# Sorted block attention followed by a PReLU layer pair: three stages in turn, or one interleaved program

## The chip, the cores and the metric

The kernel runs on one core of one Trainium2 chip. The time is the device time of one execution in microseconds (us). A profile of one execution is available, and its span runs from the first to the last recorded instruction. TensorE multiplies matrices (PE in the profile, PEld for its weight loads), VectorE is DVE, ScalarE is ACT, GpSimd is POOL and SyncE is SP. Of a matrix product, the operand that is loaded into the array is called the weights here, and the other one, whose columns stream through, the moving operand.

## The reference

Four batches, 8 heads, 768 tokens in 8 blocks of 96, head dimension 64. A small 8x8 matrix per batch and head is normalised five times and mixes the blocks of k and v; each block of queries then attends to its own mixed block; the result goes through two dense layers with a PReLU between them.

```python
for _ in range(5):                       # sort_net: [4, 8, 8, 8]
    P = np.exp(P - P.max(-1)); P = P / (P.sum(-1) + 1e-9); P = P / (P.sum(-2) + 1e-9)
k_sorted = einsum('bhij,bhjcd->bhicd', P, k_b)        # the same for v
scores = q_b @ k_sorted.T / sqrt(64); attn = softmax(scores)   # per block of 96
x = (attn @ v_sorted) as [3072 tokens, 512]
h = x @ w_in                             # 512 -> 2048
out = (maximum(h, 0) + alpha * minimum(h, 0)) @ w_out # 2048 -> 512
```

## The kernel before

The program is three stages, one behind the other, each written as a fixed order of instructions per engine (`_Plan` keeps one list per engine; the order of the calls is the order of the queues).

1. Preparation. POOL issues the loads of q, k and v, which also turn f32 into bf16, in six halves into three staging buffers `stg`. The five normalisations run on DVE with one exponential on ACT each (L178 to L196); a DMA through `L2` (L200) and a mask build the block-diagonal mixing matrix `bd_bf`. TensorE transposes q (L323) into `psKV`; k and v are mixed first (L353, evacuated at L368 and L370 into `srt`) and transposed in a second pass (L323, L389). ACT and DVE evacuate into `QT`, `KT` (L337, L339) and `VS` (L402, L404).
2. Attention, in 32 groups of one batch and one block with all 8 heads: eight score products (L510, keys in the partitions), one exponential (L519), eight products with `VS` (L539), whose 65th column of ones gives the row sum, a reciprocal (L548) and a multiplication (L554) on DVE, four transposes (L572) and their copy into `xT` (L581). The loop staggers three groups. The softmax takes no maximum off.
3. The dense layers in 6 chunks of 512 tokens: `emit_phase1` has 16 steps of four 128x512 products (L655), a Relu on ACT (L663) scaled by 1 - alpha, which is right for alpha up to 1, and a combination on DVE (L672). `emit_phase2` has 4 tiles of 16 products (L699), an evacuation on ACT (L705) and a DMA out from SP (L711). Phase 1 of a chunk is put ahead of phase 2 of the chunk before.

Of the kernel before, what the change touches and what calls it, by code (L numbers as in the profile page):

```python
# [13 lines left out]
NB = 8  # L15
# [6 lines left out]
TOK_CHUNK = 512  # L22
N_CHUNKS = NT // TOK_CHUNK
TT_PER_CHUNK = TOK_CHUNK // 128
HALF_ELEMS = 128 * 6144
NSTG = 3


class _Stream:

    def __init__(self, sem):
        self.sem = sem
        self.v = 0


class _Plan:

    ENGS = ("pool", "sync", "pe", "act", "dve")

    def __init__(self):  # L40
        self.ops = {e: [] for e in self.ENGS}

    def op(self, eng, fn, stream=None, n=1):
        if stream is None:
            self.ops[eng].append(lambda e, fn=fn: fn(e))
            return None

        def _do(e, fn=fn, s=stream.sem, n=n):
            inst = fn(e)
            inst.then_inc(s, n)  # L50
        self.ops[eng].append(_do)
        stream.v += n
        return stream.v

    def wait(self, eng, stream, value):
        if value <= 0:
            return
        sem = stream.sem
        self.ops[eng].append(lambda e, sem=sem, value=value: e.wait_ge(sem, value))


def _emit(nc, P):
    with nc.Block() as blk:
        for eng_name, starter in (("pool", blk.gpsimd), ("sync", blk.sync), ("pe", blk.tensor),
                                  ("act", blk.scalar), ("dve", blk.vector)):
            fns = P.ops[eng_name]
            if not fns:
                continue

            def _run(e, fns=fns):  # L70
                for fn in fns:
                    fn(e)
            starter(_run)


def bass_sinkhorn_attn__then__act_prelu_kernel(
    nc: bass.Bass,
    q: bass.AP,
    k: bass.AP,
    v: bass.AP,  # L80
    sort_net: bass.AP,
    moe_w_in: bass.AP,
    moe_w_out: bass.AP,
    moe_alpha: bass.AP,
    out: bass.AP,
):
    _build(nc, q, k, v, sort_net, moe_w_in, moe_w_out, moe_alpha, out, debug=None)


def _build(nc, q, k, vin, sort_net, moe_w_in, moe_w_out, moe_alpha, out, debug=None):  # L90
    P = _Plan()
    es = ExitStack()

    def sem(name):
        return es.enter_context(nc.semaphore(name))

    st_sn = _Stream(sem("s_dma_sn"))
    st_alpha = _Stream(sem("s_dma_alpha"))
    st_l2dma = _Stream(sem("s_dma_l2"))
    st_lda = [_Stream(sem("s_dma_lda%d" % i0)) for i0 in range(NSTG)]  # L100
    st_ldb = [_Stream(sem("s_dma_ldb%d" % i0)) for i0 in range(NSTG)]
    st_win = _Stream(sem("s_dma_win"))
    st_wout = _Stream(sem("s_dma_wout"))
    st_outp = [_Stream(sem("s_out0")), _Stream(sem("s_out1"))]
    st_dbg = _Stream(sem("s_dbg"))
    st_pool = _Stream(sem("s_pool"))
    st_dve = _Stream(sem("s_dve"))
    st_act = _Stream(sem("s_act"))
    st_pe = _Stream(sem("s_pe"))

    identf = es.enter_context(nc.sbuf_tensor("identf", [128, 128], F32))
    identb = es.enter_context(nc.sbuf_tensor("identb", [128, 128], BF16))
    mask128 = es.enter_context(nc.sbuf_tensor("mask128", [128, 128], F32))
    ones128 = es.enter_context(nc.sbuf_tensor("ones128", [128, 128], F32))
    P32 = es.enter_context(nc.sbuf_tensor("P32", [32, 64], F32))
# [150 lines left out]
    def issue_load(L):  # L266
        buf = L % NSTG
        readers = v_stg_readers[buf]
        if readers > 0:
            P.wait("pool", st_pe, readers)  # L270
# [485 lines left out]
```

## Time and profile before

| what | value |
|---|---|
| median of 3 runs (lowest, highest) | 314.13 us (313.93, 315.18) |
| span of the profiled execution | 312.7 us |
| mean granted TensorE clock over the span | 0.896 |
| PE, PEld busy | 279.8 us, 165.2 us |
| DVE, ACT busy | 162.6 us, 162.0 us |
| POOL busy | 10.1 us |
| moved by DMA | 20.26 MB |

The profiled execution's time outside the profiler is not recorded beside its span; the median of the runs is 1.4 us above the span. An average share over the span hides that the three stages have different limits: each stage has to be read from its own stretch of the trace. The granted clock is the share of full speed that the throttle gives to TensorE; it has a row only from the first time that it is reported.

### The profile page before, as it was taken

What the parts mean: (1) busy time and instruction counts of PE and PEld (TensorE: products, weight loads), DVE (VectorE), ACT (ScalarE), POOL (GpSimd) and SP (SyncE); (2) the same over time, 40 slices, a digit from 0 to 9 for tenths busy, and PEclk for the clock granted to TensorE, in tenths of its full rate; (3) what the DMA queues carried; (4) which work ended last, traced back from release to release, by engine and by line L of the source; (5) the groups of instructions that cost most, each with busy time, mean ns of one, the idle gap of its engine ahead of it and who ended that gap; (6) DMA issues with size and microseconds to landing.
All of it is one profiled execution on the core that took longest, in us unless ns stands there. A gap on an engine that the chain in (4) does not pass through costs nothing.

```text
span 312.7 us, 4827 instructions
## 1 busy us (share of the span) xinstructions
PE 279.8 (89%) x1950; PEld 165.2 (53%) x1970; DVE 162.6 (52%) x286; ACT 162.0 (52%) x222; POOL 10.1 (3%) x23
## 2 busy tenths in 40 slices
PE   0486788786899999978999999999999999999995
PEld 0475366445788888863444444444444444444442
DVE  5604899897466666654888108504810860482000
ACT  2498787796444444433777137516722752572111
POOL 6010300000000000001000000000000000000000
PEclk9999999999655555556999999999999999999999
DMA  6999999600000000005900020011002001100121
GB/s 83 210 215 214 214 209 212 130 2 0 2 2 0 2 0 3 2 0 79 191 0 3 34 101 0 2 74 61 2 34 84 16 3 67 67 2 34 67 100 69
DMA packets 10198, 20.26 MB, mean 65 GB/s; under 512 B 3008, under 2 KB 5056, under 8 KB 9408
## 3 DMA queue, kind: packets, MB, share of 16 engines
q0 software_dynamic: 4320, 13.63, 22.7%
q1 hardware_dynamic: 5856, 6.32, 5.9%
q8 instruction: 16, 0.26, 0.3%
q14 instruction: 6, 0.05, 0.1%
HBM read 27.28 MB, written 6.29 MB: 107 GB/s over the span
## 4 chain that ended last, share of the span: by engine, by line
PE 79%; DVE 10%; DMA 4%; ACT 3%; issue 3%; POOL 0%; SPq 0%; DVEq 0%; POOLq 0%
PE psH L655 27%; PE psO L699 26%; PE pO L539 8%; PE psS L510 8%; DMA L<-P 4%; PE psT L572 3%; PE psKV L323 3%; DVE KT L339 2%; PE ps_sort L353 2%; DVE VS L404 2%; PE psKV L389 2%; DVE QT L339 1%; ACT srt L368 1%; ACT VS L402 1%; DVE xq L554 1%
## 5 line engine op out<-in xcount | busy, mean ns | idle before, releaser
L672 DVE SCALAR_TENSOR_TENSOR hT<-psH,alphaT,t 128x512 bf16<-128x512 f32 x96 | 72.1, 751 | 69.7 <-ACT t L663 59.6
L655 PE MATMUL psH<-xT,w_in_bf 128*128 128x512 bf16 x375 | 84.7, 384 | 1.3 <-issue 0.9
L699 PE MATMUL psO<-w_out_bf,hT 128*128 128x512 bf16 x377 | 83.3, 379 | 0.4
L663 ACT ACTIVATE t<-psH,omaT 128x512 bf16<-128x512 f32 x96 | 66.0, 687 | 24.2 <-PE psH L655 24.2
L655 PEld LDWEIGHTS psH<-xT,w_in_bf 128*128 128x128 bf16 x384 | 37.9, 99 | 47.2 <-issue 3.2
L699 PEld LDWEIGHTS psO<-w_out_bf,hT 128*128 128x128 bf16 x384 | 37.6, 98 | 45.3
L705 ACT ACTIVATE outstg<-psO 128x512 f32<-128x512 f32 x24 | 14.3, 597 | 68.1 <-PE psO L699 68.1
L519 ACT ACTIVATE Esb<-psS 96x768 bf16<-96x768 f32 x32 | 25.7, 806 | 34.9 <-PE psS L510 34.9
L323 PE MATMUL psKV<-identb,stg 128*64 128x128 bf16 x192 | 17.0, 255 | 15.0 <-DVE P L196 7.4
L510 PE MATMUL psS<-QT,KT 64*96 64x96 bf16 x256 | 26.8, 274 | 1.4 <-DVE VS L404 1.4
L539 PE MATMUL pO<-VS,Esb 96*96 96x65 bf16 x256 | 26.0, 266 | 2.0 <-DVE xq L554 1.4
L539 PEld LDWEIGHTS pO<-VS,Esb 96*96 96x96 bf16 x256 | 22.6, 188 | 5.8 <-issue 1.7
L510 PEld LDWEIGHTS psS<-QT,KT 64*96 64x96 bf16 x256 | 21.9, 181 | 5.8 <-ACT VS L402 1.5
L323 PEld LDWEIGHTS psKV<-identb,stg 128*64 128x64 bf16 x192 | 14.6, 134 | 17.3 <-DMA stg<-in_q_dram 11.8
L554 DVE TENSOR_TENSOR xq<-pO,rec 96x512 bf16<-96x512 f32 x32 | 22.0, 687 | 1.1
L548 DVE RECIPROCAL rec<-pO 96x8 f32<-96x8 f32 x32 | 6.5, 204 | 25.4 <-PE pO L539 25.4
L337 ACT ACTIVATE QT<-psKV 64x1024 bf16<-64x1024 bf16 x20 | 18.7, 1022 | 1.1 <-PE psKV L323 1.0
L572 PE MATMUL psT<-identb,xq 96*128 96x96 bf16 x128 | 16.3, 278 | 1.1 <-DVE xT L581 1.1
L353 PE MATMUL ps_sort<-stg,bd_bf 128*128 128x512 bf16 x44 | 13.5, 384 | 4.0 <-DVE bd_bf L221 1.7
L368 ACT ACTIVATE srt<-ps_sort 128x512 bf16<-128x512 f32 x24 | 13.8, 594 | 2.9 <-remote 1.8
L370 DVE CAST srt<-ps_sort 128x512 bf16<-128x512 f32 x24 | 14.7, 678 | 0.8 <-PE ps_sort L353 0.8
L339 DVE COPY KT<-psKV 64x1024 bf16<-64x1024 bf16 x12 | 14.3, 1220 | 1.4 <-PE psKV L323 0.6
(45 smaller groups left out, 127.1 us busy)
## 6 DMA issues: line engine op xcount, KB each, us to landing
out_dram<-outstg SPq DMA_DIRECT2D x24, 256.0 KB, 2.0
stg<-in_q_dram POOLq DMA_DIRECT2D x2, 1280.0 KB, 13.7
stg<-in_k_dram POOLq DMA_DIRECT2D x2, 1280.0 KB, 18.5
stg<-in_v_dram POOLq DMA_DIRECT2D x2, 1280.0 KB, 11.7
w_in_bf<-in_moe_w_in_dram POOLq DMA_DIRECT2D x1, 2048.0 KB, 22.0
w_out_bf<-in_moe_w_out_dram POOLq DMA_DIRECT2D x1, 2048.0 KB, 14.4
stg<-in_q_dram POOLq DMA_DIRECT2D x2, 256.0 KB, 8.2
stg<-in_k_dram POOLq DMA_DIRECT2D x2, 256.0 KB, 12.8
```

Source lines behind the costliest of these rows:

```text
L323: inst = e.matmul(AP(psKV, (hf * 64) * 3072 + pbuf * 1024 + t * 128, [[3072, 64], [1, 128]]), AP(src_t, c * 64, [[6144, 128], [1, 64]]), i ...
L339: vv = P.op(eng, lambda e, d=dstap, s=srcap: e.tensor_copy(d, s), stream)
L353: v_mm = P.op("pe", lambda e, m=m, hf=hf, buf=buf: e.matmul(AP(ps_sort, (m % 4) * 512, [[2048, 128], [1, 512]]), AP(bd_bf, hf * 128, [[256 ...
L510: inst = e.matmul(oap, lhsT, rhs)
L519: v_exp[g] = P.op("act", lambda e, gbuf=gbuf: e.activation(AP(Esb, gbuf * 768, [[1536, 96], [96, 8], [1, 96]]), AP(psS, gbuf * 1024, [[204 ...
L539: inst = e.matmul(oap, lhsT, rhs)
L554: v_nrm[g] = P.op("dve", lambda e, gbuf=gbuf: e.tensor_tensor(out=AP(xq, gbuf * 512, [[1024, 96], [64, 8], [1, 64]]), in0=AP(pO, 0, [[1024 ...
L572: inst = e.matmul(oap, lhsT, rhs, is_transpose=True)
L655: inst = e.matmul(oap, lhsT, rhs, start=(kt == 0), stop=(kt == KT_TILES - 1))
L663: v_relu = P.op("act", lambda e, ft=ft, hbuf=hbuf: e.activation(AP(t1, hbuf * TOK_CHUNK, [[4 * TOK_CHUNK, 128], [1, TOK_CHUNK]]), AP(psH, ...
L672: v_cmb[step] = P.op("dve", lambda e, ft=ft, hbuf=hbuf, hbase=hbase: e.scalar_tensor_tensor(out=AP(hT, hbase + ft * TOK_CHUNK, [[HT_ROW, 1 ...
L699: inst = e.matmul(oap, lhsT, rhs, start=(ft == 0), stop=(ft == FT_TILES - 1))
```

## The change

The whole kernel is rewritten. `_Graph` collects every operation with what it reads and writes, an estimated duration and a priority. A list scheduler at build time then fixes the order of each engine's queue: the engine that is free earliest takes the ready operation with the lowest priority number. Copies out of PSUM may go to ACT or DVE, whichever the scheduler finds free. Waits are emitted for dependencies that are not already known to be met.

- Work goes batch by batch. Group g has priority g; the dense layers of a chunk of groups (two chunks of 192 tokens, then seven of 384) get priorities just behind the chunk's last group, so that they are placed between later groups; the preparation of the next batch is placed between the groups of the present one.
- k and v are mixed and transposed by one product each: `prep_k` has the data as weights and the mixing matrix as moving operand, 64 rows by 64 columns, two heads in two halves of the array; `prep_v` takes every 64th element of a row as a weight. q is transposed 128 columns at a time and evacuated by four copies into `QTz`, where the other head's half is zero.
- All preparation products share one PSUM bank, `psP`; `psH` has two banks in place of four, `psY` one.
- The mixing matrix is spread by a product with a selection matrix instead of a DMA. The subtraction of the maximum stays in the first normalisation alone.
- Each group computes its scores twice: once with queries in the partitions for a row maximum on DVE (`s1` and `tensor_reduce`), once with keys in the partitions, with the negative maximum added by eight more products (`s2`).
- The PReLU is h + (1 - alpha) * relu(-h): Relu with a constant scale of -1 into an f32 tile, then the combination on DVE.
- POOL also zeroes parts of `QTz` and `VST`.

The core of the diff; most removed lines stand above in the kernel before:

```diff
-TOK_CHUNK = 512
-NSTG = 3
...
-class _Plan:
...
-    for it in range(5):
-        P.wait("dve", st_dve, st_dve.v)
-        v = P.op("dve", lambda e: e.reduce_max(rm[:, :], P3, axis=AxisListType.X), st_dve)
...
-        v_l2 = P.op("sync", lambda e, hf=hf: e.dma_start(
...
-    for g in range(NG + 2):
...
-    for tc in range(N_CHUNKS):
-        emit_phase1(tc)
...
+RING = 768
...
+XLAT = {"pe": 210, "act": 60, "dve": 60, "pool": 80, "sync": 80}
...
+def t_pe(*mms):
+    return sum(max(n, m, 64) / 2.4 + 4 for n, m in mms)
...
+def t_act(n, ptr=0):
+    return 100 + n / 1.2 + 93 * ptr
...
+def t_dve(n, mode=1):
+    return 120 + n / (0.96 * mode)
...
+            best = None
+            for e in ENGS:
+                if not ready[e]:
+                    continue
+                first = max(free[e], min(o.ready[e] for o in ready[e]))
+                op = min((o for o in ready[e] if o.ready[e] <= first), key=lambda o: (o.prio, o.idx))
+                if best is None or first < best[0]:
+                    best = (first, e, op)
+            at, e, op = best
...
+    psS = ps("psS", [128, 2, 512], F32)
+    psO = ps("psO", [128, 2, 512], F32)
+    psH = ps("psH", [128, 2, 512], F32)
+    psY = ps("psY", [128, 512], F32)
+    psP = ps("psP", [128, 512], F32)
...
+        for hp in range(2):
+            G.add(POOL, lambda e, hp=hp: e.memset(
+                AP(VST[0].bitcast(F32), (hp * 64 + 32) * 3072, [[3072, 32], [1, 3072]]), 0.0),
+                3200, w=[("VST", 0, 1, hp)], prio=-80)
+        for n in range(2):
+            for hp in range(2):
+                G.add(POOL, lambda e, hp=hp, n=n: e.memset(
+                    AP(QTz[n].bitcast(F32), (1 - hp) * 64 * 3072 + hp * 1536, [[3072, 64], [1, 1536]]), 0.0),
+                    1700, w=[("QTz0", n, hp)], prio=-79 + 40 * n)
...
+            if it == 0:
+                dv(lambda e: e.reduce_max(rm[:, :], P3, axis=AxisListType.X), ["P"], ["rm"])
+                dv(lambda e: e.tensor_tensor(out=P3, in0=P3, in1=bc(rm), op=AluOpType.subtract),
+                   ["P", "rm"], ["P"])
...
+    def spread_k(b, prio):
+        G.add(PE, lambda e: e.matmul(psP[:, 0:64], AP(selk, b * 128, [[512, 32], [1, 128]]),
+                                     P32[:, :]), 500, r=["P", "selk"], w=PSP, prio=prio)
+        G.add(DVE, lambda e: e.tensor_tensor(
+            out=AP(dtmp, 0, [[64, 128], [8, 8], [1, 8]]), in0=AP(psP, 0, [[512, 128], [8, 8], [1, 8]]),
+            in1=AP(mkj, 0, [[8, 128], [0, 8], [1, 8]]), op=AluOpType.mult), 210,
+            r=PSP + ["mkj"], w=["dtmp"], prio=prio)
+        G.add(DVE, lambda e: e.reduce_sum(dsel[:, :], AP(dtmp, 0, [[64, 128], [8, 8], [1, 8]]),
+                                          axis=AxisListType.X), 200, r=["dtmp"], w=["dsel"], prio=prio)
+        G.add(DVE, lambda e: e.tensor_tensor(
...
+    def prep_q(b, u, prio):
+        n = b % 2
+        def f(e):
+            inst = None
+            for p in range(8):
+                pr = 8 * u + p
+                inst = e.matmul(AP(psPb, p * 128, [[1024, 128], [1, 128]]),
+                                AP(QS[n], pr * 128, [[3072, 128], [1, 128]]),
+                                identb[:, :], is_transpose=True)
+            return inst
+        G.add(PE, f, t_pe(*[(128, 128)] * 8), r=[("QS", n), "identb"], w=PSP, prio=prio)
+        for cp in range(2):
+            for hp in range(2):
+                o = AP(QTz[n], hp * 64 * 6144 + hp * 3072 + cp + 16 * u,
+                       [[6144, 64], [96, 32], [48, 2], [2, 8]])
+                i = AP(psPb, cp * 64 * 1024 + hp * 64, [[1024, 64], [2, 32], [1, 2], [128, 8]])
+                G.add(EITHER, lambda e, o=o, i=i: copy(e, o, i), t_either(512),
+                      r=[("psP", cp), ("QTz0", n, hp)], w=[("QTz", n, u, cp, hp)], prio=prio)
+    def prep_k(b, u, prio):
+        n = b % 2
+        def f(e):
+            inst = None
+            for c in range(8):
+                cc = 8 * u + c
+                for hp in range(2):
+                    inst = e.matmul(AP(psP, hp * 64 * 512 + c * 64, [[512, 64], [1, 64]]),
+                                    AP(KS[n], hp * 64 * 3072 + cc * 64, [[3072, 64], [1, 64]]),
+                                    AP(BDK, hp * 64 * 512 + b * 128 + hp * 64, [[512, 64], [1, 64]]))
+            return inst
+        G.add(PE, f, t_pe(*[(64, 64)] * 16), r=[("KS", n), ("BDK", b)], w=PSP, prio=prio)
+        o = AP(KT[n], 8 * u, [[3072, 128], [96, 32], [48, 2], [1, 8]])
+        i = AP(psP, 0, [[512, 128], [2, 32], [1, 2], [64, 8]])
+        G.add(EITHER, lambda e: copy(e, o, i), t_either(512), r=PSP, w=[("KT", n, u)], prio=prio)
+    def prep_v(b, u, prio):
+        n, hf, b2 = b % 2, b // 2, b % 2
+        def f(e):
+            inst = None
+            for dd in range(8):
+                inst = e.matmul(AP(psP, dd * 64, [[512, 96], [1, 64]]),
+                                AP(VST[hf], 8 * u + dd, [[6144, 128], [64, 96]]),
+                                AP(BDV, hf * 128 + b2 * 64, [[256, 128], [1, 64]]))
+            return inst
+        G.add(PE, f, t_pe(*[(64, 96)] * 8),
+              r=[("VST", hf, x, y) for x in range(2) for y in range(2)] + [("BDV", hf, b2)],
+              w=PSP, prio=prio)
+        o = AP(VS[n], 8 * u, [[64 * 65, 96], [65, 64], [1, 8]])
+        i = AP(psP, 0, [[512, 96], [1, 64], [64, 8]])
+        G.add(EITHER, lambda e: copy(e, o, i), t_either(512), r=PSP + [("VS1", n)], w=[("VS", n, u)],
+              prio=prio)
...
+        vs_keys = [("VS", n, u) for u in range(8)]
+        banks_s, banks_o = ["psS0", "psS1"], ["psO0", "psO1"]
+        def s1(e):
+            inst = None
+            for s in range(8):
+                h4, hp = s // 2, s % 2
+                inst = e.matmul(AP(psS, (s // 4) * 512 + (s % 4) * 96, [[1024, 96], [1, 96]]),
+                                AP(QTz[n], hp * 3072 + h4 * 768 + i * 96, [[6144, 128], [1, 96]]),
+                                AP(KT[n], h4 * 768 + i * 96, [[3072, 128], [1, 96]]))
+            return inst
+        G.add(PE, s1, t_pe(*[(96, 96)] * 8), r=kt_keys + qt_keys, w=banks_s, prio=prio)
+        G.add(DVE, lambda e: e.tensor_reduce(
+            AP(nm[m], 0, [[8, 96], [4, 2], [1, 4]]), AP(psS, 0, [[1024, 96], [512, 2], [96, 4], [1, 96]]),
+            AxisListType.X, AluOpType.max, negate=True), t_dve(768), r=banks_s, w=[("nm", m)], prio=prio)
+        def s2(e):
+            inst = None
+            for h4 in range(4):
+                base = (h4 // 2) * 512 + (h4 % 2) * 192
+                e.matmul(AP(psS, base, [[1024, 96], [1, 192]]),
+                         AP(KT[n], h4 * 768 + i * 96, [[3072, 128], [1, 96]]),
+                         AP(QTz[n], h4 * 768 + i * 96, [[6144, 128], [3072, 2], [1, 96]]),
+                         start=True, stop=False)
+                for hp in range(2):
+                    inst = e.matmul(AP(psS, base + hp * 96, [[1024, 96], [1, 96]]),
+                                    AP(nm[m], 2 * h4 + hp, [[8, 96], [0, 96]]),
+                                    AP(identb, 0, [[128, 96], [1, 96]]), start=False, stop=(hp == 1))
+            return inst
+        G.add(PE, s2, t_pe(*[(192, 96), (96, 96), (96, 96)] * 4), r=kt_keys + qt_keys + [("nm", m), "identb"],
+              w=banks_s, prio=prio)
+        G.add(ACT, lambda e: e.activation(
+            AP(Esb[m], 0, [[768, 96], [384, 2], [1, 384]]), AP(psS, 0, [[1024, 96], [512, 2], [1, 384]]),
+            ACTF.Exp, scale=0.125), t_act(768), r=banks_s, w=[("Esb", m)], prio=prio)
+        def o(e):
+            inst = None
+            for s in range(8):
+                h4, hp = s // 2, s % 2
+                inst = e.matmul(AP(psO, hp * 512 + h4 * 68, [[1024, 96], [1, 65]]),
+                                AP(Esb[m], s * 96, [[768, 96], [1, 96]]),
+                                AP(VS[n], ((hp * 4 + h4) * 8 + i) * 65, [[64 * 65, 96], [1, 65]]))
+            return inst
+        G.add(PE, o, t_pe(*[(65, 96)] * 8), r=vs_keys + [("Esb", m)], w=banks_o, prio=prio)
+        G.add(DVE, lambda e: e.reciprocal(AP(rec[m], 0, [[8, 96], [4, 2], [1, 4]]),
+                                          AP(psO, 64, [[1024, 96], [512, 2], [68, 4]])), 200,
+              r=banks_o, w=[("rec", m)], prio=prio)
...
+        def tr(e):
+            inst = None
+            for kt in range(4):
+                inst = e.matmul(AP(psOb, 640 + kt * 96, [[2048, 128], [1, 96]]),
+                                AP(xq[m], kt * 128, [[512, 96], [1, 128]]),
+                                AP(identb, 0, [[128, 96], [1, 96]]), is_transpose=True)
+            return inst
+        G.add(PE, tr, t_pe(*[(96, 128)] * 4), r=[("xq", m), "identb"], w=["psO0"], prio=prio)
+        o2 = AP(xT, b * S + i * BLK, [[KT_TILES * NT, 128], [NT, 4], [1, 96]])
+        i2 = AP(psOb, 640, [[2048, 128], [96, 4], [1, 96]])
+        G.add(EITHER, lambda e: copy(e, o2, i2), t_either(384, 2), r=["psO0"], w=[("xT", g)], prio=prio)
...
+    def ffn1(ga, gb, ft, prio):
+        tok, n = ga * BLK, (gb - ga) * BLK
+        hb, tb = step[0] % 2, step[0] % 3
+        step[0] += 1
...
+        G.add(PE, f, t_pe(*[(n, 128)] * 4), r=[("xT", g) for g in range(ga, gb)] + [("w_in", ft // 4)],
+              w=[("psH", hb)], prio=prio)
+        G.add(ACT, lambda e: e.activation(AP(t1[tb], 0, [[384, 128], [1, n]]),
+                                          AP(psH, hb * 512, [[1024, 128], [1, n]]), ACTF.Relu, scale=-1.0),
+              t_act(n), r=[("psH", hb)], w=[("t1", tb)], prio=prio)
+        G.add(DVE, lambda e: e.scalar_tensor_tensor(
+            out=AP(hT, ft * RING + tok % RING, [[FT_TILES * RING, 128], [1, n]]),
+            in0=AP(t1[tb], 0, [[384, 128], [1, n]]), scalar=AP(omaT, ft, [[16, 128], [1, 1]]),
+            in1=AP(psH, hb * 512, [[1024, 128], [1, n]]), op0=AluOpType.mult, op1=AluOpType.add),
+            t_dve(n), r=[("psH", hb), ("t1", tb), "omaT"],
...
+    def ffn2(t, prios):
+        tok = t * 128
+        if t < 21:
+            bank, key, row = (psY, 0), "psY", 512
+        else:
+            bank, key, row = ((psS, (t % 2) * 512), "psS%d" % (t % 2), 1024)
+        ob = t % 4
...
+    for u in range(3):
+        prep_q(0, u, -50)
+    for b in range(4):
+        spread_k(b, -48 if b == 0 else 1.0 + b)
+        if b % 2 == 0:
+            spread_v(b // 2, -47 if b == 0 else 1.5 + b)
+        if b == 0:
+            for u in range(6):
+                prep_k(0, u, -46)
+            for u in range(8):
+                prep_v(0, u, -45)
...
+    chunks = [(0, 2), (2, 4)] + [(c, c + 4) for c in range(4, NG, 4)]
+    tile_done = 0
+    ffn_plan = []
+    for ga, gb in chunks:
+        w = gb - ga
+        v0 = gb + 0.5
+        for ft in range(FT_TILES):
+            ffn_plan.append((v0 + w * ft / FT_TILES, 0, (ga, gb, ft)))
+        last = gb * BLK // 128
+        nt = last - tile_done
+        for x in range(nt):
+            prios = [v0 + w + w * (x + p / 4) / nt for p in range(4)]
+            ffn_plan.append((prios[0], 1, (tile_done + x, prios)))
...
+        b, i = g // NB, g % NB
+        if i == 0 and b + 1 < B:
+            load_k(b + 1, 8 * b - 20)
+            if b != 2:
+                load_v(b + 1, 8 * b - 19)
+            if b == 1:
+                load_v(3, 8 * b - 17)
+            load_q(b + 1, 8 * b - 18)
+        attention(g, g)
+        if b + 1 < B:
+            units = ([(prep_k, u) for u in range(6)] + [(prep_v, u) for u in range(8)]
+                     + [(prep_q, u) for u in range(3)])
+            for x in range(len(units)):
+                if i == 1 + x * 7 // len(units):
+                    units[x][0](b + 1, units[x][1], 8 * b + 1 + x * 7 / len(units) - 2)
...
```

More of the change, by code (lines that the diff above doesn't have):

```diff
@@ L62, in _emit @@
[L62 to L73, printed above, removed]
+NG = B * NB
+RING = 768
+EPS = 1e-9
+XLAT = {"pe": 210, "act": 60, "dve": 60, "pool": 80, "sync": 80}
```

965 lines of the change are left out of this document (374 added, 591 removed).

## The prediction

> **What bounds the kernel now.** I read the page's first two parts, then the busy time by stretch with its clock, then the timeline at the borders of the stages. The columns of a stretch are its length, busy us (and instructions) of PE, PEld, DVE, ACT and POOL, granted clock, DMA share, GB/s.
>
> ```profile
> span 312.7 us, 4827 instructions
> PE 279.8 (89%) x1950; PEld 165.2 (53%) x1970; DVE 162.6 (52%) x286; ACT 162.0 (52%) x222; POOL 10.1 (3%) x23
> ...
> PEclk9999999999655555556999999999999999999999
> DMA  6999999600000000005900020011002001100121
> ...
> 0.00:19.30 19.30, 7.76 (x72) 7.52 (x73) 8.90 (x41) 9.11 (x14) 4.96 (x15) 1.00 0.89 160
> 19.30:79.00 59.70, 45.58 (x506) 30.70 (x508) 44.56 (x53) 47.80 (x59) 3.95 (x7) 1.00 0.71 143
> 79.00:141.00 62.00, 59.53 (x623) 51.36 (x624) 36.74 (x95) 24.82 (x31) 0.00 (x0) 0.51 0.01 1
> 141.00:145.50 4.50, 3.62 (x12) 1.42 (x12) 1.11 (x2) 0.76 (x2) 1.16 (x1) 0.50 0.23 25
> 145.50:309.60 164.10, 163.26 (x745) 74.17 (x758) 71.32 (x95) 78.95 (x119) 0.00 (x0) 1.00 0.18 50
> ```
>
> There are three limits. Preparation takes 79 us, with no engine full: the loads fill the DMA for seven slices of 7.8 us, and ACT and DVE evacuate. Attention takes 62 us with PE busy throughout, but at half the clock. The dense layers take 164 us at full clock with no gap. So 164 us can't shrink; what can is the 145 us ahead, in which TensorE is idle, small-grained or slow. The clock has no event before 19.3 us, so the 1.00 of the first stretch is no measurement; the durations say what it was:
>
> ```profile
> 13.46 6.50 PE L323 MATMUL psKV<-identb,stg 128*64 128x128 bf16 x64 [4.14 <-DMA stg<-in_q_dram]
> 20.17 0.47 PEld L323 LDWEIGHTS psKV<-identb,stg 128*64 128x64 bf16 x8 [0.38 <-ACT QT L337]
> 20.18 0.63 PE L323 MATMUL psKV<-identb,stg 128*64 128x128 bf16 x8 [0.22 <-ACT QT L337]
> 21.09 0.63 PE L323 MATMUL psKV<-identb,stg 128*64 128x128 bf16 x8 [0.28 <-ACT QT L337]
> 79.00 0.43 PEld L539 LDWEIGHTS pO<-VS,Esb 96*96 96x96 bf16 x8 [0.66 <-ACT Esb L519]
> ...
> 87.51 0.71 PEld L510 LDWEIGHTS psS<-QT,KT 64*96 64x96 bf16 x8
> ...
> 142.20 8.07 PE L655 MATMUL psH<-xT,w_in_bf 128*128 128x512 bf16 x29 [0.88 <-issue]
> ...
> L510 PEld LDWEIGHTS psS<-QT,KT x16: 116/122/122, 77.9 to 79.8; 64*96 64x96 bf16 x16
> ```
>
> At 13.46 us, 64 transposes take 0.102 us each; at 20.17 us eight loads take 0.47 us, about 0.05 each. The start runs at half clock too.
>
> **The change, part by part.** It makes one PE-bound program of the three, so the sum is: PE's work at full clock, plus the time before PE can be kept full, plus what it loses.
>
> *PE's work.* From the last stretch, a 512-column product costs 164.1/758 = 0.2165 us. Eight loads of 96 columns take 0.43 us, the last of them 0.122: (0.43 - 0.122)/7 = 0.044 each. A 128-column transpose is 0.05, a 192-column product 0.2165 x 192/512 = 0.081.
> - Dense layers: the same columns, 768 x 0.2165 = 166.3, and 192 more instructions by narrower chunks; I take 167 us.
> - Attention, per group: `s1` 8 x 0.044 = 0.35; `s2` 8 x 0.044 + 4 x 0.081 = 0.68 (this is the added pass for the maximum); output 0.35; transposes 4 x 0.05 = 0.20. Together 1.58, times 32 = 51 us. Before it was 62 us at half clock, so the doubled scores are paid by the clock, if the clock is full.
> - Preparation: q 96 x 0.05 = 5 us. k 384 products of 64x64: between 0.022 (two halves of the array at once) and 0.044 (the 96-column row); I take 0.035, 13.4 us (8.4 to 17). v 256 products, whose weights are every 64th element: between 0.044 and 0.084 ((0.71 - 0.12)/7, the same load at half clock, as the worst near row); I take 0.05, nearest to the contiguous row, 12.8 us (11.3 to 21.5). With the spreads 32 us. The old second pass of transposes for k and v goes.
>
> [...]
>
> PE total: 167 + 51 + 32 = 250 us.
>
> *The time until PE is full.* The dense layers can start when two groups are in `xT`.
>
> ```profile
> 2.82 0.21 DVE L178 TENSOR_REDUCE rm<-P 32x8 f32<-32x64 f32 x1
> 3.31 0.26 ACT L183 ACTIVATE P<-P 32x64 f32<-32x64 f32 x1 [1.22 <-DVE P L180]
> ...
> 14.01 0.26 DVE L196 TENSOR_TENSOR P<-P,cs 32x64 f32<-32x64 f32 x1
> ...
> 14.98 11.62 DMA L<-P
> ...
> L137 POOL MEMSET ones<- 128x128 f32 x1 | 0.2, 204 | 0.3 <-POOLq L741 0.3
> L741 POOL MEMSET const-float32-0.0<- 128x1 f32 x1 | 0.1, 98 | 0.3 <-issue 0.3
> 10.00:20.00 10.00, 6.50 (x64) 6.33 (x64) 3.21 (x15) 7.76 (x11) 0.00 (x0) 1.00 1.01 206
> 140.35 0.34 DVE L581 COPY xT<-psT 128x384 bf16<-128x384 bf16 x1
> 140.81 0.29 PEld L572 LDWEIGHTS psT<-identb,xq 96*128 96x128 bf16 x4 [1.24 <-DVE xT L581]
> 140.84 0.48 PE L572 MATMUL psT<-identb,xq 96*128 96x96 bf16 x4 [1.05 <-DVE xT L581]
> 141.36 0.36 DVE L581 COPY xT<-psT 128x384 bf16<-128x384 bf16 x1 [0.66 <-PE psT L572]
> L370 DVE CAST srt<-ps_sort 128x512 bf16<-128x512 f32 x24 | 14.7, 678 | 0.8 <-PE ps_sort L353 0.8
> L368 ACT ACTIVATE srt<-ps_sort 128x512 bf16<-128x512 f32 x24 | 13.8, 594 | 2.9 <-remote 1.8
> ```
>
> The normalisation ended at 14.3 us; four maxima and subtractions of 3.31 - 2.82 = 0.49 go, one short operation comes: 12.5 us. The 11.6 us of the `L` DMA, queued behind the loads, go. The loads of q, k, v of batch 0 are 2.36 MB, 11.5 us at 206 GB/s, now first in POOL's queue: in by 15 us. POOL's zeroing: 0.098 + 0.83 ns per column gives 2.65 us for 3072 and 1.4 us for 1536, so two and two end near 11.5 us, and the copies into `QTz` wait for them.
>
> From there one bank, `psP`, takes everything in turn, at half clock (sparse products did not raise it before). Bank free to first load: 0.12 us (140.69 to 140.81). Last product's tail plus hand-over: 0.25 (four products at 0.09 end at 141.32, the copy starts at 141.36). A copy of 512: 0.6 to 0.68. So a unit of k costs 16 x 0.06 + 0.37 + 0.64 = 1.97; of v 8 x 0.084 + 0.37 + 0.69 = 1.73; of q, with four copies on two engines, 8 x 0.102 + 0.37 + 1.28 = 2.5. One q unit waits for the zeroing and ends at 12.3; two more to 17.3; two spreads of 0.75 to 18.8; six of k to 30.6; eight of v to 44.5. Then two groups' output, scaling, transposes and copy, about 2.9 us each, in turn on `psO`: 50 us. At full clock the same chain is 2.1, 1.57 and 1.46 us a unit and 2.4 us a group: 44 us.
>
> By then PE has done a quarter of the preparation (8), three groups' scores (3), two groups' rest (1) and some units of batch 1 (1): 13. Left: 237 us.
>
> *What is lost behind 50 us.* The clock has to rise; before, it rose 3.3 us after dense products began (142.20 to 145.5), and I take 5 us at half, 2.5 lost (0 to 5). ACT and DVE must keep up:
>
> ```profile
> L672 DVE SCALAR_TENSOR_TENSOR hT<-psH,alphaT,t 128x512 bf16<-128x512 f32 x96 | 72.1, 751 | 69.7 <-ACT t L663 59.6
> L519 ACT ACTIVATE Esb<-psS 96x768 bf16<-96x768 f32 x32 | 25.7, 806 | 34.9 <-PE psS L510 34.9
> L554 DVE TENSOR_TENSOR xq<-pO,rec 96x512 bf16<-96x512 f32 x32 | 22.0, 687 | 1.1
> L548 DVE RECIPROCAL rec<-pO 96x8 f32<-96x8 f32 x32 | 6.5, 204 | 25.4 <-PE pO L539 25.4
> L581 DVE COPY xT<-psT 128x384 bf16<-128x384 bf16 x32 | 11.0, 344 | 0.7 <-PE psT L572 0.7
> L339 DVE COPY KT<-psKV 64x1024 bf16<-64x1024 bf16 x12 | 14.3, 1220 | 1.4 <-PE psKV L323 0.6
> L705 ACT ACTIVATE outstg<-psO 128x512 f32<-128x512 f32 x24 | 14.3, 597 | 68.1 <-PE psO L699 68.1
> 309.59 0.60 ACT L705 ACTIVATE outstg<-psO 128x512 f32<-128x512 f32 x1 [2.86 <-PE psO L699]
> out_dram<-outstg SPq DMA_DIRECT2D x24, 256.0 KB, 2.0
> ```
>
> A column costs DVE (1.220 - 0.678)/512 = 1.06 ns and ACT (0.806 - 0.597)/256 = 0.82 ns. The combination of 384 is then 0.615, of 192 0.41: 112 and 32 of them make 82 us. The new row maximum of 768 is 0.678 + 256 x 1.06 ns = 0.95, times 32 = 30. With scaling (22), reciprocals (6.5) and the start (10) DVE has 151. ACT has Relu 112 x 0.49 + 32 x 0.34 = 66 and exponentials 26: 92. Copies for either: 104 in preparation (68), 24 out (14), 32 to `xT` (13): 95. Together 338 us, 169 per engine, of which about 146 (all but the preparation of batch 0, the start and three groups) fall in the dense stretch of 237: 62%. The cover is there on average.
>
> Two-bank `psH` gives a step each (0.65 + 0.25 + 0.49 + 0.1 + 0.615 + 0.12)/2 = 1.1 us, against 237/32 = 7.4 us of PE work for a group's four steps. The group's own chain, `s1`, maximum, `s2`, exponential, is about 3.6 us, under 7.4. Each wait in PE's queue now holds all that is behind it, other stages' products too; where an ACT or DVE operation is late, PE stands. The order is made with 520 ns for a combination that I put at 615 and 740 for the exponential that took 806, so some are late; but dense products mostly stand between. I take 5 us (0 to 30).
>
> *The end.* Last product to end of span is 312.7 - 309.6 = 3.1 us, the copy and a DMA of 2.0; unchanged.
>
> **Sum:** 50 + 237 + 2.5 + 5 + 3.1 = 297.6 us of span against 312.7. The median of the runs stands 1.4 us above the span, so 299 us.
>
> **Rivals.**
> 1. *Quicker start* (chance 0.2). If `psP` runs at full clock or the zeroing is not in the way, the start is 44; with the k products in pairs (-5) and no stall (-5): 299 - 6 - 5 - 5, about 283; without the clock's loss 280. For it: eight loads take 0.43 once the clock is up. Against: nothing dense precedes.
> 2. *Slower: PE's fixed order waits for ACT and DVE* (0.14). If before each `s2` one combination (0.615) stands in DVE's queue unforeseen, and before each output product one Relu (0.49), PE loses 1.1 us a group, 35 us: 299 - 5 + 35 = 329. It passes the time before at 20 us in all, 0.63 us a group. For it: priorities place a group's products the moment they are ready by an optimistic table. Against: 62% load, and work from other stages in front.
> 3. *Clock lost* (0.08). At 87.51 us PE was busy without a break, and the clock stayed at half for 60 us: small products don't raise it. If a fifth of the stretch runs at half clock, 237/0.9 = 263, 26 more in place of 2.5: 323. Against: it held at eight 128-column transposes per 0.91 us (20.18, 21.09), 1024 columns where 2150 fit, 48%; the new mix has two thirds dense products. [...]
> 4. *Work is not interleaved* (0.05): attention runs first and the dense layers are left over; 32 groups at 4 us with PE 85% full would lose 19 us, 299 - 5 + 19 = 313: no change.
>
> **How the numbers follow.** My forecast, 286 to 311 by its own bounds, has 0.53. Range 279 to 320: below lies a part of rival 1, above most of 2 and 3, about 0.2. A measurement of this kernel can tell 0.5%, 1.6 us. Faster: 0.53 + 0.2 + 0.03 of rival 4 = 0.76; same 0.06 (the rest of 4, the mild ends of 2 and 3); slower 0.18, the remainder of 2 and 3.
>
> **What would show it.** PE's first dense product near 50 us; `psP` products and copies alternating with nothing between from 12 to 45 us at clock 0.5; clock 1.0 within 7 us of the first dense products, and to the end; PE over 95% busy from there; the last dense layers without attention over some 30 us; DVE and ACT near 169 us each. I would be wrong if waits of PE on DVE sum to over 20 us, if the clock falls again, or if `L572`-like chains on `psO` hold the groups above 7.4 us.

## The result, and the profile after

The changed kernel took 328.97 us (median of four runs, 328.4 to 329.65) against 314.65 us (313.93 to 315.98) before: 1.0453 times as long, 95% interval 1.042 to 1.0485. The forecast was 299 us, faster than before; the kernel is 4.5% slower. The profiled execution has a span of 326.5 us, where the sum of the prediction gave 297.6. Times here are medians of all executions; ratios and their intervals leave out the few slow ones, among them one of 914.58 us of the kernel with its copies on ACT.

From the page of the changed kernel: the span, the engines, PE over 40 slices of 8.2 us, the chain that ended last by engine and by line, and the load of the v weights among the costliest groups (busy us, mean ns of one, then the idle time before).

```profile
span 326.5 us, 6224 instructions
PE 287.7 (88%) x2696; PEld 208.7 (64%) x2733; DVE 185.7 (57%) x363; ACT 154.0 (47%) x285; POOL 24.4 (7%) x34
...
PE   0014688999998999999999999999999999999996
...
PE 82%; DVE 9%; ACT 5%; issue 2%; POOL 1%; POOLq 0%
...
L468 PEld LDWEIGHTS psP<-BDV,VST 128*96 128x96 bf16 x256 | 44.6, 255 | 3.9 <-ACT VS L289 1.4
```

The program is what it was meant to be: PE is full from slice 8 to the end and carries 82% of the chain. DVE and ACT together are busy 339.7 us, where the prediction had 338. So the question is not who holds PE up, but why PE has more to do and begins late. `L468` answers the first half: the 256 loads for v keep the weight path busy for 44.6 us, in a term of the sum that had 12.8.

Busy time of each engine by stretch (length, then PE, PEld, DVE, ACT, POOL busy and their instructions, clock, DMA share, GB/s), changed kernel:

```profile
50.00:68.00 18.00, 16.84 (x131) 15.36 (x131) 9.02 (x25) 5.24 (x9) 0.99 (x2) 1.00 0.66 133
68.00:310.00 242.00, 237.87 (x2301) 169.94 (x2336) 151.50 (x275) 130.61 (x246) 1.10 (x2) 1.00 0.10 30
```

From 68 us on PE is idle for 4.1 us of 242. As before, the 1.00 ahead of the first clock event says nothing. The start, in the timeline (start, length, engine, line):

```profile
5.57 2.65 POOL L330 MEMSET VST<- 32x3072 f32 x1
5.85 2.65 DVE L352 COPY selk<-identf 32x512 f32<-32x512 f32 x1
...
8.43 3.23 DVE L357 COPY selv<-identf 32x64 f32<-32x64 f32 x4
8.95 2.65 POOL L330 MEMSET VST<- 32x3072 f32 x1
9.00 2.66 DVE L375 TENSOR_REDUCE rm<-P 32x8 f32<-32x64 f32 x1
...
14.58 1.38 POOL L335 MEMSET QTz<- 64x1536 f32 x1
...
18.07 0.73 ACT L289 ACTIVATE QTz<-psP 64x512 bf16<-64x512 bf16 x1
...
22.14 1.04 PE L432 MATMUL psP<-identb,QS 128*128 128x128 bf16 x8 [13.24 <-DVE QTz L289]
...
22.63 0.26 DVE L389 TENSOR_TENSOR P<-P,cs 32x64 f32<-32x64 f32 x1
...
25.92 1.51 DVE L289 COPY QTz<-psP 64x512 bf16<-64x512 bf16 x2 [1.19 <-PE psP L432]
...
27.58 0.65 PE L393 MATMUL psP<-P,selk 32*128 32x64 f32 x2 [1.70 <-DVE QTz L289]
...
29.55 0.64 PE L453 MATMUL psP<-BDK,KS 64*64 64x64 bf16 x16 [0.32 <-DVE dtmp L410]
...
30.88 0.64 PE L453 MATMUL psP<-BDK,KS 64*64 64x64 bf16 x16 [0.69 <-ACT KT L289]
...
37.51 1.38 PEld L468 LDWEIGHTS psP<-BDV,VST 128*96 128x96 bf16 x8 [0.82 <-ACT KT L289]
...
56.68 0.85 PE L525 MATMUL psO<-VS,Esb 96*96 96x65 bf16 x8 [0.77 <-ACT VS L289]
...
65.59 1.46 PE L562 MATMUL psH<-xT,w_in_bf 128*128 128x192 bf16 x8
...
68.25 0.44 PE L453 MATMUL psP<-BDK,KS 64*64 64x64 bf16 x16
68.63 0.50 PE L562 MATMUL psH<-xT,w_in_bf 128*128 128x192 bf16 x4
...
118.81 1.38 PEld L468 LDWEIGHTS psP<-BDV,VST 128*96 128x96 bf16 x8
```

The normalisation ended at 22.9 us (predicted 12.5), the first dense product ran at 65.6 (predicted 50), and the clock rose about 68.2: eight 192-column products took 1.46 us before, and 16 k products 0.64 before and 0.44 after. A unit of eight v loads took 1.38 us on both sides of that step.

### The profile page after: what moved, and what is told of

It is laid out like the page before. It is cut to its first block, busy times and chain, and to the rows that moved or that the text cites. A ratio compares the mean times of both kernels' runs of the same rounds, so it can differ in the third digit from the quotient of the medians.

```text
span 326.5 us, 6224 instructions
## 1 busy us (share of the span) xinstructions
PE 287.7 (88%) x2696; PEld 208.7 (64%) x2733; DVE 185.7 (57%) x363; ACT 154.0 (47%) x285; POOL 24.4 (7%) x34
## 3 DMA queue, kind: packets, MB, share of 16 engines
q0 software_dynamic: 5728, 13.63, 22.5%
## 4 chain that ended last, share of the span: by engine, by line
PE 82%; DVE 9%; ACT 5%; issue 2%; POOL 1%; POOLq 0%
PE psH L562 24%; PE psY L594 20%; PE psP L468 13%; PE psO L525 4%; PE psS L506 4%; PE psS L511 4%; PE psS L493 3%; PE psP L453 3%; PE psS L594 3%; DVE QTz L289 3%; PE psO L542 2%; ACT QTz L289 1%; PE psP L432 1%; ACT KT L289 1%; DVE selv L357 1%
## 5 line engine op out<-in xcount | busy, mean ns | idle before, releaser
L573 DVE SCALAR_TENSOR_TENSOR hT<-t,omaT,psH 128x384 bf16<-128x384 f32 (+1 forms) x144 | 80.1, 564 | 54.5 <-ACT t L570 53.9
L562 PE MATMUL psH<-xT,w_in_bf 128*128 128x384 bf16 (+1 forms) x576 | 102.1, 310 | 0.2
L570 ACT ACTIVATE t<-psH 128x384 f32<-128x384 f32 (+1 forms) x144 | 64.7, 453 | 67.3 <-PE psH L562 66.4
L594 PE MATMUL psY<-w_out_bf,hT 128*128 128x512 bf16 x300 | 78.3, 379 | 2.6 <-issue 0.8
L594 PEld LDWEIGHTS psY<-w_out_bf,hT 128*128 128x128 bf16 x336 | 31.2, 100 | 26.2 <-DVE hT L573 0.3
L468 PEld LDWEIGHTS psP<-BDV,VST 128*96 128x96 bf16 x256 | 44.6, 255 | 3.9 <-ACT VS L289 1.4
L468 PE MATMUL psP<-BDV,VST 128*96 128x64 bf16 x256 | 45.5, 326 | 1.8 <-ACT VS L289 0.8
L498 DVE TENSOR_REDUCE nm<-psS 96x8 bf16<-96x768 f32 x32 | 30.5, 952 | 17.6 <-PE psS L493 16.4
L506 PE MATMUL psS<-QTz,KT 128*96 128x192 bf16 x128 | 27.6, 267 | 0.1
L511 PE MATMUL psS<-identb,nm 96*96 96x96 bf16 x256 | 27.6, 219 | 0.0
L289 ACT ACTIVATE QTz<-psP 64x512 bf16<-64x512 bf16 x25 | 18.8, 752 | 5.2 <-PE psP L432 4.7
## 6 DMA issues: line engine op xcount, KB each, us to landing
VST<-in_v_dram POOLq DMA_DIRECT2D x8, 384.0 KB, 18.8
```

The costliest lines, as they stand in the source:

```text
L289: return e.activation(o, i, ACTF.Copy) if e is nc.scalar else e.tensor_copy(o, i)
L468: inst = e.matmul(AP(psP, dd * 64, [[512, 96], [1, 64]]), AP(VST[hf], 8 * u + dd, [[6144, 128], [64, 96]]), AP(BDV, hf * 128 + b2 * 64, [[ ...
L498: G.add(DVE, lambda e: e.tensor_reduce(AP(nm[m], 0, [[8, 96], [4, 2], [1, 4]]), AP(psS, 0, [[1024, 96], [512, 2], [96, 4], [1, 96]]), Axis ...
L506: e.matmul(AP(psS, base, [[1024, 96], [1, 192]]), AP(KT[n], h4 * 768 + i * 96, [[3072, 128], [1, 96]]), AP(QTz[n], h4 * 768 + i * 96, [[61 ...
L511: inst = e.matmul(AP(psS, base + hp * 96, [[1024, 96], [1, 96]]), AP(nm[m], 2 * h4 + hp, [[8, 96], [0, 96]]), AP(identb, 0, [[128, 96], [1 ...
L562: inst = e.matmul(AP(psH, hb * 512, [[1024, 128], [1, n]]), AP(w_in_bf, kt * DFF + ft * 128, [[KT_TILES * DFF, 128], [1, 128]]), AP(xT, kt ...
```

## The experiments

Two causes were put to the test: the loads of v, whose 96 columns lie 64 elements apart, are the missing PE time; and the start is late by the order in DVE's queue and by copies there that end with POOL's zeroing. Against them stood that PE waits for ACT and DVE, and that interleaving itself costs more than it brings. Gains are told against the changed kernel's 328.97 us; the kernel before took 314.6 to 315.1 us beside each experiment, so the runs can be set side by side.

**v weights from contiguous columns.**

```
-  AP(VST[hf], 8 * u + dd, [[6144, 128], [64, 96]]),
+  AP(VST[hf], (8 * u + dd) * 96, [[6144, 128], [1, 96]]),
```

> The 96 weights of each v product lie side by side in place of every 64th element, with the same order of instructions; the v values that are mixed are then the wrong ones. Theory A (strided weight loads cost PE's time): a v product goes from 0.15-0.17 us to 0.045 at full clock and 0.085 at half; 192 of them in the dense stretch give 20 us, 64 at the start give 5: about 304 us (300 to 309). Rival B (v products are long because they wait for psP or for ACT and DVE): 324 us or more, and the loads in the trace stay above 0.12 us each.

Measured: 304.05 us, 0.9642 of before (0.9585 to 0.97). One stride in one access pattern makes the slower kernel a faster one (it then mixes other values of v, with the same instructions); 24.9 us of the time went. The timeline of this kernel (one unit at half clock, one at full), and then its loads behind 80 us (min/median/max ns):

```profile
37.49 0.71 PEld L468 LDWEIGHTS psP<-BDV,VST 128*96 128x96 bf16 x8 [0.83 <-ACT KT L289]
...
109.98 0.44 PEld L468 LDWEIGHTS psP<-BDV,VST 128*96 128x96 bf16 x8
```

```profile
L468 PEld LDWEIGHTS psP<-BDV,VST x168: 120/125/126, 80.1 to 185.9; 128*96 128x96 bf16 x168
```

The same view of the changed kernel:

```profile
L468 PEld LDWEIGHTS psP<-BDV,VST x185: 238/257/260, 79.9 to 210.0; 128*96 128x96 bf16 x185
```

With the prediction's own way of taking the last load off, a load costs (0.44 - 0.125)/7 = 0.045 us from contiguous columns and (1.38 - 0.257)/7 = 0.160 strided, 3.6 times as much. The 192 units' loads that lie behind the start make 192 x 0.115 = 22 us, and batch 0 gave 4.1 (first dense product 61.49 against 65.59). Together 26, and the span fell by 24.2.

**What in the stride costs: every 4th and every 8th element.** The same edit with `[4, 96]` and with `[8, 96]`, one run each.

> The same with every 4th element (8 bytes). [...] Rival B (any distance but one is dear): 0.15 us a load and 328 us.

> The v weights are taken every 8th element (16 bytes) in place of every 64th (128 bytes); the v values mixed are the wrong ones. [...] Rival B (the cost comes from the long distance, or from 128 bytes being a bad multiple): 0.05 to 0.09 us a load, 304 to 314 us.

Measured: 311.98 and 331.06 us. Timelines, stride 4 and then stride 8, each with the median of its loads behind it:

```profile
112.88 0.80 PEld L468 LDWEIGHTS psP<-BDV,VST 128*96 128x96 bf16 x8
```

```profile
L468 PEld LDWEIGHTS psP<-BDV,VST x171: 162/187/190, 79.9 to 193.6; 128*96 128x96 bf16 x171
```

```profile
119.96 1.49 PEld L468 LDWEIGHTS psP<-BDV,VST 128*96 128x96 bf16 x8
```

```profile
L468 PEld LDWEIGHTS psP<-BDV,VST x188: 249/272/274, 79.8 to 212.7; 128*96 128x96 bf16 x188
```

That is 0.088 us at stride 4 and 0.174 at stride 8, against 0.160 at 64. So distance isn't the price: with the columns 16 and 128 bytes apart a load costs about the same, and with 8 bytes half of that, which is still twice the 0.045 of the contiguous load. Rival B missed at both strides: it gave 0.05 to 0.09 us a load and 304 to 314 us at stride 8, 0.15 us and 328 us at stride 4. What in the memory or in the load sets these prices is not shown, and no other stride was run.

**Start: the copies into `selk` and `selv` on ACT.** Nothing else is moved.

```
-  G.add(DVE, lambda e: e.tensor_copy(AP(selk, ...
+  G.add(ACT, lambda e: copy(e, AP(selk, ...
...
-  G.add(DVE, lambda e, hf=hf, hp=hp: e.tensor_copy(
+  G.add(ACT, lambda e, hf=hf, hp=hp: copy(e,
```

> The change as it is, with the copies of the selection matrices on ACT in place of DVE and nothing else moved. Theory A (DVE's copies of 2.65 and 3.2 us are long because POOL's zeroing of 2.65 us holds them, and the normalisation stands behind them): its first reduction ends near 5.9 us in place of 11.7, the normalisation ends 3 to 6 us earlier, and the time falls by 2 to 5 us: 324 to 327. Rival B (the zeroing of QTz bounds the q units whatever DVE does): under 1 us.

Measured: 323.95 us, 1.0292 of before (1.0268 to 1.0317). Timeline of this kernel, ACT, DVE and PE:

```profile
4.84 0.63 ACT L289 ACTIVATE selk<-identf 32x512 f32<-32x512 f32 x1 [2.75 <-POOL identf L324]
...
5.86 0.20 DVE L375 TENSOR_REDUCE rm<-P 32x8 f32<-32x64 f32 x1
...
24.39 0.64 PE L453 MATMUL psP<-BDK,KS 64*64 64x64 bf16 x16 [0.32 <-DVE dtmp L410]
```

In the changed kernel the copy into `selk` ended just behind POOL's zeroing beside it (5.57 + 2.65 = 8.22; 5.85 + 2.65 = 8.50), the copies into `selv` just behind the next one (11.60; 11.66), and the reduction of the maximum, which stands behind the copies, at 11.66 too. With the copies on ACT, where the one into `selk` takes 0.63 us, the reduction takes 0.20 us and ends at 6.06 beside the same zeroing, the first k product is 5.2 us earlier, and the time is 5.0 us shorter. That the zeroing held these copies on DVE is read from the ends that coincide; no run has them on DVE without zeroing beside them. The 2.66 us of the reduction in the changed kernel would then be its time behind the copies.

**Start: all that holds it.** The copies as above, the small loads ahead in the scheduler's model of the DMA queue, and `QTz` of batch 0 zeroed before `VST`.

```
-  begin = max(dma_free, free[e] + 700)
+  begin = free[e] + 700 if dur <= 300 else max(dma_free, free[e] + 700)
...
+  ... w=[("QTz0", n, hp)], prio=-79 + 40 * n)
```

> The scheduler no longer queues the two small loads behind q, k and v, so that the normalisation stands first in DVE's queue; the selection matrices are copied by ACT in place of DVE; POOL zeroes QTz ahead of VST. Theory A (the start is a chain of DVE behind POOL's zeroing, normalisation, psP): the normalisation ends near 13 us in place of 22.9, the first k product begins near 17 in place of 29.5, and the time falls by 10 to 13 us: 316 to 319. Rival B (the loads bound the start: v of batch 0 and w_in arrive late): the first k product moves, the first dense product does not, and the time stays above 325 us.

Measured: 322.62 us, 1.0252 of before (1.0183 to 1.032), 6.4 us gained and not the 10 to 13 expected. DVE in this kernel:

```profile
7.16 0.25 DVE L390 TENSOR_REDUCE cs<-P 32x8 f32<-32x64 f32 x1
9.59 0.75 DVE L290 COPY QTz<-psP 64x512 bf16<-64x512 bf16 x1 [2.17 <-PE psP L438]
10.23 0.17 DVE L394 RECIPROCAL cs<-cs 32x8 f32<-32x8 f32 x1
```

The normalisation began at 2.5 us, but the written order has the copies of q between its steps; the first waits 2.17 us for PE, and a reciprocal that depends on nothing of it stands behind. The normalisation ended at 20.06 us. So the wait of 2.17 us in DVE's queue also held the reciprocal, which needed nothing of what was waited for. The first k product came 7.4 us earlier, and 6.4 us of that reached the end.

**The row maximum left out.** `s1`, the reduction into `nm` and the two products that subtract it are gone.

> The row maximum is left out: no first score pass, no reduction, no products that add the negative maximum. Theory A (PE bounds the stretch from 68 us on): 32 x (8 + 8) products of 0.044 us and some change of order go, 23 us: 303 to 309. Rival B (DVE or the group's chain of waits bounds the stretch): less than 8 us, as PE only idles more. Rival C (the chain of a group matters too): more than 30 us.

Measured: 306.44 us, 0.9753 of before (0.968 to 0.9827): 22.5 us less, 0.70 us a group. The prediction's prices had 0.35 for `s1` and 0.36 for the subtraction, 0.71. So that term was sized right, it is paid in PE time, and it is not hidden.

**Dense layers last.** The first dense layer waits for all 32 groups, so nothing is interleaved.

```
-  r=[("xT", g) for g in range(ga, gb)] + [("w_in", ft // 4)],
+  r=[("xT", g) for g in range(NG)] + [("w_in", ft // 4)],
...
-  while fp < len(ffn_plan) and ffn_plan[fp][0] < g:
+  while g >= NG and fp < len(ffn_plan) and ffn_plan[fp][0] < g:
```

> Every dense product also waits for all 32 groups, so that the dense layers are not interleaved; all else as changed. Theory A (interleaving keeps PE full and its clock up): attention with its chain of about 4 to 4.8 us a group from 57 us on, at half clock for most of it, then 170 us of dense layers: 370 to 390 us. Rival B (interleaving gives little, the sum of PE's work decides): under 345 us, with the clock at full in attention.

Measured: 433.76 us, 1.3765 of before (1.3641 to 1.3888), 105 us more than interleaved and more than expected. Busy time by stretch, and then the timeline of PE:

```profile
70.00:255.00 185.00, 145.25 (x1412) 129.77 (x1411) 70.69 (x119) 67.40 (x103) 1.09 (x2) 1.00 0.05 10
```

```profile
256.00 1.46 PE L562 MATMUL psH<-xT,w_in_bf 128*128 128x192 bf16 x8 [0.23 <-DVE hT L573]
...
258.93 0.82 PE L562 MATMUL psH<-xT,w_in_bf 128*128 128x192 bf16 x8
```

The step from 1.46 to 0.82 us is the first rise of the clock: the whole of attention ran at half (16 k products took 0.63 us at 76.15, eight products with `VS` 0.86 at 249.65), and PE was idle for 40 us of these 185. Within this kernel, interleaving is thus worth far more than the change lost elsewhere; it was not the culprit. (The kernel before, which doesn't interleave either, needs 62 us for its attention, whose groups do less.)

**Everything at once.** The early start, no row maximum, and the v weights put side by side by copies into a ring `VSR`: in batch 0 on ACT and DVE, later on POOL. To make room, `t` is in bf16 and the output has three buffers, and the scheduler's model lands loads 2.2 us later.

```
+  G.add(eng, lambda e: copy(e, AP(VSR, 768 * (u % 4), [[3072, 128], [96, 8], [1, 96]]),
+                            AP(VST[hf], 8 * u, [[6144, 128], [1, 8], [64, 96]])), dur,
...
-  AP(VST[hf], 8 * u + dd, [[6144, 128], [64, 96]]),
+  AP(VSR, (8 * (u % 4) + dd) * 96, [[3072, 128], [1, 96]]),
```

> A version from the findings: v is put side by side by copies ahead of its products (batch 0 on ACT and DVE, later batches on POOL, which is idle), the start is reordered as in the early-start run with the loads modelled 2.2 us later, and the row maximum is left out. By the sum of the single runs: 329 - 25 (v) - 6.4 and some more (start) - 22.5 (maximum) + 2 (copies) = 275 to 280 us. [...]

Measured: 275.70 us, 0.8759 of before (0.8735 to 0.8782). The parts add up: 329.0 - 24.9 - 22.5 - 6.4 = 275.2. The stride is now paid by POOL, whose idle time before these copies is, by the page of this kernel, a wait for PE and not the other way round:

```profile
L291 POOL COPY VSR<-VST 128x768 bf16<-128x768 bf16 x24 | 36.3, 1512 | 51.2 <-PE psP L482 48.6
```

The same with the row maximum, so that nothing of the change is left out:

> The same with the row maximum kept: 22 us more than the combined version, 297 to 302 us, under the 314.6 of before. Rival (DVE, which carries the maximum, becomes the bound once PE's work is cut): over 306 us.

Measured: 294.64 us, 0.9367 of before (0.9342 to 0.9391), a little under what was expected. The maximum costs 18.9 us here and cost 22.5 alone, so it is in part chance that the sum above meets the time within 0.5 us; the smaller edits (`t` in bf16, three buffers, the modelled landing) were not run alone.

**Products without use in the gaps of the start.** In batch 0, between PE's sparse units, two 512-column products each, to raise the clock.

```
+  inst = e.matmul(psY[:, :], identb[:, :], AP(QS[0], x * 512, [[3072, 128], [1, 512]]))
+  G.add(PE, f, t_pe(*[(512, 128)] * 2), r=PSP + [("QS", 0), "identb"], w=["psY"], prio=prio)
```

> The combined version with two extra 512-column products (result unused) behind each unit of batch 0 at the start, in the time in which psP is being copied out. Theory A (the start runs at half clock only because its products are sparse): the clock event comes before 40 us in place of 56.5, units of k and v get 0.2 to 0.3 us shorter, the first dense products run at full clock, and the time falls by 3 to 7 us: 269 to 273 us. Rival B (the clock can't be raised there, or the start is bound by copies alone): the event stays above 50 us, or the time stays at 274 us or more.

Measured: 286.42 us, 0.9105 of before (0.9069 to 0.9141): 10.7 us slower than without. PE in this kernel:

```profile
21.62 0.64 PE L460 MATMUL psP<-BDK,KS 64*64 64x64 bf16 x16 [0.32 <-DVE dtmp L417]
22.95 1.03 PE L614 MATMUL psY<-QS,identb 128*128 128x512 bf16 x2 [0.69 <-ACT KT L291]
23.91 0.63 PE L460 MATMUL psP<-BDK,KS 64*64 64x64 bf16 x16
...
45.38 0.51 PE L482 MATMUL psP<-BDV,VSR 128*96 128x64 bf16 x8
46.66 0.65 PE L614 MATMUL psY<-QS,identb 128*128 128x512 bf16 x2 [0.77 <-ACT VS L291]
47.10 0.82 PE L482 MATMUL psP<-BDV,VSR 128*96 128x64 bf16 x8
```

The products wait for the copy out of `psP` (0.69 us), and the next unit stands behind them: 2.29 us a unit where it was 1.33. They filled no gap, they lengthened the chain: the first dense product came at 59.95 us, without them at 50.69. The clock did rise, at about 40 us, and fell again at 47.1, where the products with `VSR` go from 0.51 to 0.82 us, although a pair still stood in each unit of 1.72 us. The time is as rival B had it, but not because the clock can't be raised. Then the dependence on `psP` was replaced by one on PE's order alone (`r=[("QS", 0), "identb"], w=["psY", "seq"]`; the units write `seq` too):

> The combined version without row maximum (275.7 us) with two more 512-column products in each unit of the first batch, as in e7_filler, but ordered on TensorE alone: they run while psP is copied out, and the next unit's first product no longer waits behind them. Their results are not used. Theory A (the clock rises once TensorE is busy for long enough, and the start is then paid at full clock): the clock event of 1.0 comes before 40 us and no event of half follows, the first dense product comes before 48 us, and the time is 267 to 273 us. Theory B (the clock does not follow the filler, or the copies out of psP bound the start whatever the clock): no full clock before 50 us or a fall back to half after it, and 275 us or more.

Measured: 270.83 us, 0.8612 of before (0.8591 to 0.8633), the best of all. PE in this kernel:

```profile
25.63 0.63 PE L460 MATMUL psP<-BDK,KS 64*64 64x64 bf16 x16
26.20 1.02 PE L614 MATMUL psY<-QS,identb 128*128 128x512 bf16 x2
27.14 0.44 PE L460 MATMUL psP<-BDK,KS 64*64 64x64 bf16 x16
27.52 0.60 PE L614 MATMUL psY<-QS,identb 128*128 128x512 bf16 x2
...
40.01 0.60 PE L614 MATMUL psY<-QS,identb 128*128 128x512 bf16 x2
...
43.66 0.55 PE L522 MATMUL psO<-VS,Esb 96*96 96x65 bf16 x8 [0.22 <-ACT xT L291]
...
46.88 0.85 PE L522 MATMUL psO<-VS,Esb 96*96 96x65 bf16 x8
47.88 1.46 PE L559 MATMUL psH<-xT,w_in_bf 128*128 128x192 bf16 x8
```

The clock rose at about 27 us. It was lost again at about 44, some 3.5 us after the last added pair, before the dense products had begun, and the second condition that was named (no fall) failed. Even so 4.9 us were gained, 2.8 of them ahead of the first dense product (47.88 against 50.69). What lost the clock is not shown: in the run before, it fell with pairs still in their places. From rise to fall it is about 17 us here and 7 us there; how long before the fall its cause lies is not shown either.

## Why the prediction was wrong

**The span, term by term.** It is 326.5 - 297.6 = 28.9 us too long. Ahead of the first dense product 15.6: the first k product came at 29.55 and not 18.8 (+10.8), the k units took 8.0 and not 11.8 (-3.8), the v units 19.2 and not 13.9 (+5.3), and from there to the dense layers 8.9 and not 5.5 (+3.4). Behind it 13.3: the strided loads of three batches, 192 x (0.160 - 0.05) = +21.1; k, which ran as if in pairs at (68.63 - 68.25)/16 = 0.024 and not 0.035, 288 x 0.011 = -3.2; the clock, up 2.6 us after the first dense product, -1.2; and -3.4 in stalls and small differences that I did not part further.

**The step that failed first: the price of v.** The prediction said 12.8 us with 11.3 to 21.5 as bounds, "nearest to the contiguous row". 256 loads at 0.160 are 41 us. The upper bound was a contiguous load at half clock, which has nothing to do with a stride: no row of before showed a strided weight load, so no row could bound it. The runs show 0.160 us a load, 3.6 times the contiguous 0.045. With the v term right, and nothing else, the sum is 297.6 + 21.1 behind the start + 5.3 in batch 0's units = 324, against a span of 312.7 before: a loss to forecast.

**The second: the time until PE is full.** The zeroing that batch 0's `QTz` needs was said to end at 11.5; it ended at 15.96. Its four memsets took the 8.1 us that were counted, but POOL began them at 5.57 and not at the 3.4 that an end at 11.5 implies, and issued three loads between them (2.3 us in all). The first copy into `QTz` started at 18.07, behind the normalisation's exponentials on ACT, and the others stood between the normalisation's steps: the first q unit was copied out at 22.1 and not 12.3, and PE waited 13.24 us for it. From there to the first k product it took 7.5 us against 6.5. The normalisation, said to end at 12.5, ended at 22.9: it began behind the copies into `selk` and `selv`, and then alternated with q's copies. But the spreads did not wait for its end, they waited for the third q unit's copies (25.92 + 1.51 = 27.43); it cost time by standing in the same queues. The prediction counted each chain by itself and did not read the order in which the list scheduler had put the two into one queue. Moving the copies alone returned 5.0 us of this.

**What was right.** The dense layers and attention together cost about what the sum said (the part tested alone, the maximum, 0.70 us a group against 0.71); work on DVE and ACT came to 339.7 us against 338; the clock rose within 7 us of the first dense products and stayed, in the profiled execution; PE lost 4.1 us in the dense stretch against 5. Taken with contiguous loads the kernel made 304.05 us, inside the forecast's own 286 to 311, in part by chance: its first dense product was still 11.5 us late (61.49 against 50), and what follows was 6.8 us shorter than the sum had it. The signs by which the prediction would have known itself wrong watched waits and the clock. PE's waits for DVE came to 17.7 us, under the 20 named, and the clock held; no sign watched the length of a load.

**The rivals.** The second rival gave 329 us, and 329 was measured. It was still wrong: it had PE waiting 35 us for ACT and DVE, and from 68 us on PE waited for 4.1 us in all (the 17.7 us for DVE lie almost wholly ahead of the first k product). The number agreed because another term was off by about as much. The third (clock lost) fell by the clock, the fourth by the interleaving: the fully separate order took 433.76 us.

## What to carry to other kernels

Look at the innermost stride of every weight operand before counting it as a load: at 96 columns of bf16, two bytes out of each 16 or each 128 cost 3.9 and 3.6 times the contiguous load here (0.174 and 0.160 us against 0.045), and a copy by an idle engine, even one of 1.5 us per 768 columns, pays for it. Where a price shows in no row of the profile, don't bound it by a row that differs in something else; give the unknown its own wide range, and work out from which value the sign of the result turns. In a single written order, read each engine's queue around the start instruction by instruction: an early chain ends where its neighbours in the queue let it.

## What the runs showed that was not expected

- A strided unit of eight loads took 1.38 us at half clock (37.51 us) and 1.38 at full (118.81), while the contiguous unit went from 0.71 to 0.44. At a stride of 64, TensorE's clock was not what limited it.
- PE busy for 145 us of 185 left the clock at half while the products were small (before, 59.5 of 62 us), and a pair of 512-column products in each unit of 1.5 us raised it. Being busy in the profile's sense was not enough here. How much work holds the clock is not shown: it fell about 3.5 us after the last added pair in one run, and with a pair in each unit of 1.72 us in the other.
- The 64x64 products ran as if in pairs, on two halves of the array: 16 in 0.64 us at half clock, 0.04 each, where two thirds of a contiguous 96-column load at that clock (0.71/8 us) would be 0.06.
